# Longer warming, earlier raw weights, two more large tiles and joined read-backs at the start of an FFT and two expert layers

## The chip, the cores and the metric

One core of a Trainium2 chip runs the whole program. Its engines are TensorE (PE; its weight loads are PEld), VectorE (DVE), ScalarE (ACT), GpSimd (POOL) and SyncE (SP, which here only issues DMA transfers). The metric is the device time of one execution in microseconds.

## The reference

```python
def reference(x, moe_w_in, moe_w_out, moe2_w_in, moe2_w_out, moe2_alpha):
    X = fft(fft(x, axis=1), axis=2).real          # x: (2, 3008, 256)
    x = X.reshape(6016, 256)
    h = x @ moe_w_in                              # 256 x 2048
    x = (h * sigmoid(h)) @ moe_w_out              # 2048 x 256
    h = x @ moe2_w_in
    return (max(h, 0) + moe2_alpha * min(h, 0)) @ moe2_w_out
```

A two-dimensional Fourier transform of each of two batches (only its real part is kept) is followed by an expert layer with SiLU and one with a leaky rectifier whose slope differs by column.

## The kernel before, in words

**The transform.** 3008 is 64 times 47. Stage A folds the input (mirrored rows and columns are added and subtracted on VectorE and GpSimd) and multiplies by the 64-point cosines and sines (`psa`); the result `ya` is written to memory as `ys`, in three parts of the output index (`K_PARTS`: 12, 12 and 8 of 32) for each of two halves `h`, and is read back in another layout as `y`, since stage B needs 96 other rows on the partitions. In stage B (`psb`) the 47-point transform is done, one small matmul for each output index; its result is split into a high part by ScalarE and a low part by VectorE (`z`). Stage C transforms the 256 columns in three products, `ce`, `co` and `cn`, giving the even and odd parts (`eo`) of a pair of mirrored tokens. A batch has three chunks of 502 pairs.

**The expert layers.** For each chunk and each of 16 blocks of the hidden dimension (96 steps in all) there are six matmuls `pe` and `po`, VectorE forms `t`, `hp = t + po` and `t - po`, ScalarE applies SiLU, one engine takes the low half `gl`, and twelve matmuls add to the output. The first two chunks run side by side, blocks 0 to 7 of each and then 8 to 15. The second layer follows with a scheme of seven products in place of eight.

**Precision and weights.** A product in full precision is made of three matmuls of high and low parts. Weights arrive as 64-bit floats; a raw piece is turned into 32-bit floats by one ScalarE and four VectorE operations (`cvi`, `cvo`; lines 181, 185, 189, 193 and 197). A group of weights `g` is a quarter of the hidden dimension; `load_w1(g)` and `load_o1(g)` load its raw inputs and outputs, `load_half` does it by halves for group 0.

**Order.** The start, up to stage C of chunk 0, is written in order by hand (`manual_schedule`): on each engine, SP's queue included, instructions run in that order. From there a planner with its own estimate of times orders the instructions of the 96 steps; `PLAN` says at which step each piece is put into its list, and it may set an instruction earlier, in the head too. `behind(st, 0)` holds a step's instructions behind chunk 0's last ScalarE step on that engine. `warm` issues matmuls whose result nobody reads, 12 calls of it after stage A; a call in full 32-bit precision is two passes. Large tiles (8 KB in each partition: x, `ya`, `y`, `z`, `eo`, raw weights) share 10 slots of the pool `bp`; a transfer into a tile waits until the tile that had the slot before is no longer used.

The order of SP's queue at the place of the change is: stores of `ys` part 0, first half of raw outputs of group 0, `y` part 0, second half of those, `ys` part 1, `y` part 1, raw inputs of group 1, alpha, `ys` part 2, raw outputs of group 1, `y` part 2.

Of the kernel before, what the change touches and what calls it, by code (L numbers as in the profile page):

```python
# [25 lines left out]
PLAN = {  # L26
# [5 lines left out]
}  # L32
# [15 lines left out]
F_PARTS = (0, 8, 16)  # L48
ORDER = [(c, f) for f0, f1 in zip(F_PARTS, F_PARTS[1:]) for c in range(2) for f in range(f0, f1)]
ORDER += [(c, f) for c in range(2, NC) for f in range(NF)]  # L50
WARM = 12
WARM0 = 8
SUM0 = "vpapap"
I1_AT = 0
# [11 lines left out]
FA0, FR0, R0, RS0, CD0, SD0, SG0, OD0, NCONST = 0, 128, 256, 444, 634, 762, 890, 1018, 1146  # L66


def _tables():
    c = np.zeros((128, NCONST), np.float64)  # L70
    n1 = np.arange(N1)
    th = 2 * np.pi * np.outer(n1, np.arange(33)) / N1
    fa = np.zeros((N1, 64))
    fa[:, :32] = np.cos(th[:, :32])
    fa[:, 32] = np.cos(th[:, 32])
    fa[:, 33:] = np.sin(th[:, 1:32])
    fr = fa.copy()
    fr[:, 1:32] = -fa[:, 33:]
    fr[:, 33:] = fa[:, 1:32]
    for q in range(2):  # L80
        for j in range(2):
            for k0, k1 in zip(K_PARTS, K_PARTS[1:]):
                at = 4 * k0 + (2 * q + j) * (k1 - k0)
                for to, f in ((FA0, fa), (FR0, fr)):
                    c[64 * q : 64 * q + 64, to + at : to + at + k1 - k0] = f[:, 32 * j + k0 : 32 * j + k1]
    n2 = np.arange(24)
    ph = 2 * np.pi * np.outer(n2, np.arange(N2)) / N2
    co, si = np.cos(ph), np.sin(ph)
    row = 4 * (n2 % 12) + 2 * (n2 // 12)
    for h, (re, im) in enumerate(((co, -si), (si, co))):  # L90
        for j in range(2):
            for to, at in ((R0 + 94 * h, 47 * j), (RS0 + 95 * h, 48 if j else None)):
                if at is None:
                    c[row, to : to + 24] = re[:, :24]
                    c[row + 1, to + 24 : to + 48] = re[:, :24]
                else:
                    c[48 * j + row, to + at : to + at + 47] = re
                    c[48 * j + row + 1, to + at : to + at + 47] = im
    m = np.arange(128)
    ps = 2 * np.pi * np.outer(m, m) / D  # L100
    c[:, CD0 : CD0 + 128] = np.cos(ps)
    c[0, CD0 : CD0 + 128] = 1 - m % 2
    c[:, SD0 : SD0 + 128] = -np.sin(ps)
    c[:, SG0 : SG0 + 128] = ((-1.0) ** m)[:, None]
    c[0, OD0 : OD0 + 128] = m % 2
    return c.astype(np.float32)
# [13 lines left out]
def fft_moe_kernel(  # L120
# [12 lines left out]
    nc = tc.nc  # L133
    wp = ctx.enter_context(tc.tile_pool(name="wp", bufs=1))
    dp = ctx.enter_context(tc.tile_pool(name="dp", bufs=1, space=bass.MemoryType.DRAM))
    bp = ctx.enter_context(tc.tile_pool(name="bp", bufs=10))
    ep = ctx.enter_context(tc.tile_pool(name="ep", bufs=3))
    cp = ctx.enter_context(tc.tile_pool(name="cp", bufs=5))
    kp = ctx.enter_context(tc.tile_pool(name="kp", bufs=16))
# [24 lines left out]
    def split(hi, lo, src, lo_eng=None):  # L164
        nc.scalar.activation(hi, src, AF.Copy)
        return (lo_eng or nc.vector).tensor_tensor(lo, src, hi.bitcast(F32), op=ALU.subtract)
# [57 lines left out]
    cs = wp.tile([128, CD0], F32, tag="cs", name="cs")  # L224
    fh = wp.tile([128, 128], F32R, name="fh")
    fl = wp.tile([128, 128], F32R, name="fl")
# [5 lines left out]
    YS = {}  # L232
    Y = {}
# [72 lines left out]
    def load_y(b, h, kh):  # L306
        w = (K_PARTS[kh + 1] - K_PARTS[kh]) // 2
        if (b, kh) not in Y:
            Y[b, kh] = big([96, 2, 6, 128], F32, f"y{b}_{kh}")
        src = YS[b, h, kh].rearrange("n (a j k) m -> j (n a) k m", a=4, j=2)  # L310
        for j in range(2):
            last = nc.sync.dma_start(Y[b, kh][48 * j : 48 * j + 48, h, :w, :], src[j])
        return last

    def stage_b(b, h):
        at = [0]
# [80 lines left out]
    def load_half(key, src, i, at=None):  # L397
        if key not in RAW:
            RAW[key] = big([128, 1024, 2], U32, f"raw_{key}")
        at = i * 512 if at is None else at  # L400
        t = RAW[key].rearrange("p n t -> p (n t)")
        return nc.sync.dma_start(t[:, i * 1024 : i * 1024 + 1024], src[:, at : at + 512].bitcast(U32))
# [9 lines left out]
    def load_w1(g):  # L412
        load_raw(f"i{g}", wi1[0, :, 512 * g : 512 * g + 512], wi1[1, :, 512 * g : 512 * g + 512])

    def load_o1(g):
        load_raw(f"o{g}", wo1[:, 1024 * g : 1024 * g + 1024])
# [361 lines left out]
    def warm(w, x, n):  # L778
        if n == 0:
            return  # L780
        ps = mm_ps("warm")
        for j in range(n):
            nc.tensor.matmul(ps[:, : x.shape[1]], w, x, start=True, stop=True)

    if True:
        with tc.manual_schedule():
            zero = conv(F32, "zero")
            nc.vector.memset(zero[:, :256], 0.0)
            warm(zero[:, :128], zero[:, :256], WARM0)
            nc.vector.memset(sm, 0.0)  # L790
            nc.scalar.activation(sm[:1, :1], sm[:1, :1], AF.Silu)
            for j in range(len(PIECES) - 1):
                load_x(0, j, (PIECES[j + 1] - PIECES[j]) // 2)
                if j == 0:
                    nc.sync.dma_start(cs[:, :R0], cst[:, :R0])
            cc = conv(F32, "cc")
            for g in range(2):
                load_half("i0", wi1[g], g, 0)
                if g == 0:
                    nc.sync.dma_start(cc, cst[:, CD0:])  # L800
                    nc.sync.dma_start(w128_raw.rearrange("p n t -> p (n t)"), w128.bitcast(U32))
            nc.sync.dma_start(cs[:, R0:], cst[:, R0:CD0])
            fold, mm, rest = stage_a(0)
            (i00, _), (i01, after_i0) = prep_w1(0)
            for (h, i), n in zip(A_ORDER, A_WARM):
                if h == 0:
                    fold(i)
                mm(h, i)
                warm(cs[:, FA0 : FA0 + 128], cs[:, :256], n)
            load_half("o0", wo1, 0)  # L810
            for h in range(2):
                load_y(0, h, 0)
            load_half("o0", wo1, 1)
            warm(cs[:, FA0 : FA0 + 128], cs[:, :256], WARM)
            (s0, p0), (s1, p1) = prep_o1(0)
            w128_st = to_f32(lambda: w128_sb, ("w128", 0, NF), "w128")[1]
            run(i00[:4])
            run(i01[:2])
            run(w128_st[:1])
            nc.scalar.activation(ch, cc, AF.Copy)  # L820
            run(i00[4:])
            for ab in zip(i01[2:], w128_st[1:]):
                run(ab)
            run(w128_st[4:])
            nc.vector.tensor_tensor(cl, cc[:, : SG0 - CD0], ch.bitcast(F32)[:, : SG0 - CD0], op=ALU.subtract)
            for n, (st, pool) in enumerate(zip(after_i0, SUM0)):
                (st if callable(st) else st[pool == "v"])()
                if n == 2:
                    run(s0)
            b00, b01 = stage_b(0, 0), stage_b(0, 1)  # L830
            run(b00[:2])
            run(b01[:2])
            run(p0)
            run(s1[:EARLY_O0])
            run(stage_c(0, 0))
            rest(1)
            for h in range(2):
                load_y(0, h, 1)
            load_w1(1)
            nc.sync.dma_start(alpha_sb, alpha)  # L840
            rest(2)
            load_o1(1)
            for h in range(2):
                load_y(0, h, 2)
        n1 = NC * NF
# [9 lines left out]
        def put(a, b, steps):  # L855

            for j, st in enumerate(steps):
                plan.setdefault(a + (b - a) * j // len(steps), []).append(st)
# [5 lines left out]
        def behind(st, *at):  # L864
            with ExitStack() as stack:
                for k in at:
                    stack.enter_context(tc.issue_after(LAST[k].ins))
                run([st])
# [4 lines left out]
                nc.gpsimd.tensor_copy(cx[64 * j : 64 * j + 1, :], ch[:1, OD0 - CD0 : OD0 - CD0 + 128])  # L873

        put(*PLAN["cx"], [mixed_cosines])
        put(*PLAN["fa"], [lambda: split(fh, fl, cs[:, FA0 : FA0 + 128])])
        put(*PLAN["o0"], [lambda st=st: behind(st, 0, ("low", 0)) for st in s1[EARLY_O0:] + p1])
        put(*PLAN["i1"], [lambda st=st: behind(st, 0, ("t", I1_AT)) for st in staged(prep_w1(1))])
        put(*PLAN["o1"], staged(prep_o1(1)))
# [11 lines left out]
        a, b = PLAN["w2"]  # L891
# [19 lines left out]
        with tc.manual_schedule():  # L911
            low1(n1 - 1)
            for n in range(NP + 2):
                run(plan.pop(n1 + n, []))
                t, p = divmod(n, 8)
# [93 lines left out]
```

## Time and profile before

| | |
|---|---|
| median of 3 runs | 984.3 us (981.82 to 985.46) |
| profiled execution | 988.99 us, span 987.2 us |
| TensorE busy | 957.9 us, 97% of the span |
| VectorE, ScalarE, GpSimd busy | 780.8, 710.7, 405.4 us |
| mean granted clock of TensorE | 0.988 of full speed |

The span runs from the first instruction to the last one. The granted clock is the share of its full speed that TensorE was given; 1.00 is 2.4 GHz and 0.50 is 1.2 GHz. In the chain of work that ended last, TensorE has 78%, VectorE 9%.

### The profile page before, as it was taken

What the parts mean: (1) busy time and instruction counts of PE and PEld (TensorE: products, weight loads), DVE (VectorE), ACT (ScalarE), POOL (GpSimd) and SP (SyncE); (2) the same over time, 40 slices, a digit from 0 to 9 for tenths busy, and PEclk for the clock granted to TensorE, in tenths of its full rate; (3) what the DMA queues carried; (4) which work ended last, traced back from release to release, by engine and by line L of the source; (5) the groups of instructions that cost most, each with busy time, mean ns of one, the idle gap of its engine ahead of it and who ended that gap; (6) DMA issues with size and microseconds to landing.
All of it is one profiled execution on the core that took longest, in us unless ns stands there. A gap on an engine that the chain in (4) does not pass through costs nothing.

```text
span 987.2 us, 14338 instructions
## 1 busy us (share of the span) xinstructions
PE 957.9 (97%) x5170; PEld 824.7 (84%) x5170; DVE 780.8 (79%) x1328; ACT 710.7 (72%) x1410; POOL 405.4 (41%) x355
## 2 busy tenths in 40 slices
PE   7889899999999999999899999999999999999998
PEld 5768787888878788787789999999999999999997
DVE  6888898676796876958687887878878788787876
ACT  3557566665667666666887888878888788787875
POOL 2677869333257467697641221312213122131200
PEclk9789999999999999999999999999999999999999
DMA  8730300230110201100000000000000000000000
GB/s 264 235 122 3 105 22 1 52 104 1 43 43 9 94 1 43 43 9 35 1 1 22 1 22 22 1 21 1 21 9 14 21 1 21 2 22 21 1 21 21
DMA packets 16614, 37.05 MB, mean 38 GB/s; under 512 B 1824, under 2 KB 11296, under 8 KB 14880
## 3 DMA queue, kind: packets, MB, share of 16 engines
q1 hardware_dynamic: 16544, 36.15, 11.1%
q8 instruction: 40, 0.66, 0.3%
q14 instruction: 30, 0.25, 0.1%
HBM read 26.83 MB, written 9.31 MB: 37 GB/s over the span
## 4 chain that ended last, share of the span: by engine, by line
PE 78%; DVE 9%; issue 5%; POOL 4%; ACT 3%; DMA 1%; SPq 0%; POOLq 0%; ACTq 0%; DVEq 0%
PE a L768 27%; PE ac L670 20%; PE a L610 5%; PE a L612 5%; PE a L608 5%; PE b L670 3%; POOL gl L588 2%; PE po L560 1%; PE po L561 1%; PE pe L560 1%; PE po L562 1%; DVE hp L571 1%; PE pe L562 1%; PE pe L561 1%; PE psb L325 1%
## 5 line engine op out<-in xcount | busy, mean ns | idle before, releaser
L768 PE MATMUL a<-gh,wo 128*128 128x502 f32 x768 | 268.2, 391 | 0.0
L588 POOL TENSOR_TENSOR gl<-t,gh 128x502 fp32r<-128x502 f32 x96 | 131.6, 1371 | 95.1 <-ACT t L576 81.6
L768 PEld LDWEIGHTS a<-gh,wo 128*128 128x128 f32 x768 | 145.0, 189 | 23.2
L737 DVE SCALAR_TENSOR_TENSOR h<-h,fc,q 128x502 f32<-128x502 f32 x192 | 130.3, 679 | 38.4 <-ACT q L732 35.7
L610 PE MATMUL a<-gl,wo 128*128 128x502 f32 x384 | 148.3, 395 | 4.1 <-POOL gl L588 4.1
L768 PE MATMUL a<-gl,wo 128*128 128x502 f32 x384 | 149.7, 391 | 0.0
L612 PE MATMUL a<-gh,wo 128*128 128x502 f32 x384 | 147.3, 393 | 0.0
L748 DVE TENSOR_TENSOR gl<-h,gh 128x502 fp32r<-128x502 f32 x192 | 140.5, 732 | 0.1
L575 ACT ACTIVATE gh<-hp 128x502 fp32r<-128x502 f32 x96 | 59.7, 622 | 92.6 <-DVE hp L571 90.6
L608 PE MATMUL a<-gh,wo 128*128 128x502 f32 x384 | 122.8, 397 | 1.2 <-ACT gh L575 0.8
L743 ACT ACTIVATE gh<-h 128x502 fp32r<-128x502 f32 x192 | 118.5, 617 | 2.1 <-DVE h L737 2.1
L732 ACT ACTIVATE q<-h,fc 128x502 f32<-128x502 f32 x192 | 116.9, 609 | 3.0 <-DVE h L715 1.5
L646 POOL TENSOR_TENSOR xt<-o 128x252 f32<-128x252 f32 x24 | 16.7, 716 | 187.2 <-ACT q L732 131.1
L568 DVE SCALAR_TENSOR_TENSOR t<-n,sm,pe 128x502 f32<-128x502 f32 x96 | 70.2, 731 | 29.0 <-PE pe L562 25.3
L610 PEld LDWEIGHTS a<-gl,wo 128*128 128x128 f32 x384 | 73.2, 191 | 20.7 <-POOL gl L588 5.9
L588 POOL TENSOR_TENSOR gl<-hp,gh 128x502 fp32r<-128x502 f32 x52 | 69.4, 1335 | 47.6 <-ACT hp L576 39.8
L571 DVE TENSOR_TENSOR hp<-t,po 128x502 f32<-128x502 f32 x96 | 64.5, 672 | 29.5 <-PE po L562 23.8
L608 PEld LDWEIGHTS a<-gh,wo 128*128 128x128 f32 x384 | 72.2, 191 | 17.5 <-ACT gh L575 2.2
L612 PEld LDWEIGHTS a<-gh,wo 128*128 128x128 f32 x384 | 73.1, 190 | 15.0
L768 PEld LDWEIGHTS a<-gl,wo 128*128 128x128 f32 x384 | 72.5, 189 | 7.7
L704 ACT ACTIVATE u<-ac 128x252 f32<-128x252 f32 x96 | 36.6, 381 | 51.6 <-PE ac L670 51.6
L656 POOL TENSOR_TENSOR os<-o,os 128x252 fp32r<-128x252 f32 x36 | 32.5, 918 | 94.5 <-ACT os L655 92.6
(191 smaller groups left out, 2296.0 us busy)
## 6 DMA issues: line engine op xcount, KB each, us to landing
out_t<-ot SPq DMA_DIRECT2D x24, 251.0 KB, 2.5
x<-in_xs SPq DMA_DIRECT2D x8, 512.0 KB, 5.6
raw_i<-in_wi SPq DMA_DIRECT2D x8, 512.0 KB, 4.7
raw_w<-in_wi SPq DMA_DIRECT2D x4, 1024.0 KB, 5.0
raw_w<-in_wo SPq DMA_DIRECT2D x4, 1024.0 KB, 4.8
raw_o<-in_wo SPq DMA_DIRECT2D x3, 1024.0 KB, 5.6
y<-ys SPq DMA_DIRECT2D x16, 144.0 KB, 2.9
x<-in_xs SPq DMA_DIRECT2D x2, 1024.0 KB, 4.8
```

What stands on the lines that cost most here:

```text
L568: nc.vector.scalar_tensor_tensor(t, E128[c], w128_sb[:, f : f + 1], pe, op0=ALU.mult, op1=ALU.add)
L571: nc.vector.tensor_tensor(hp, t, po, op=ALU.add)
L588: (nc.gpsimd if s or lo_pool(i + 1) else nc.vector).tensor_tensor(lo, h, hi.bitcast(F32), op=ALU.subtract)
L608: nc.tensor.matmul(ACC1[lb, s], hi, G[i, s][0], start=st, stop=False)
L610: nc.tensor.matmul(ACC1[lb, s], hi, G[i, s][1], start=False, stop=False)
L612: nc.tensor.matmul(ACC1[lb, s], lo, G[i, s][0], start=False, stop=sp)
L670: nc.tensor.matmul(to, w, x, start=start and q == 0, stop=q == 2, skip_group_check=True)
L732: nc.scalar.activation(h["q", i][:, to], source(n, part), AF.Abs, scale=coef(n, i, 1))
L737: nc.vector.scalar_tensor_tensor(h[f"h{i}"][:, to], source(n, part), coef(n, i, 0), h["q", i][:, to], op0=ALU.mult, op1=ALU.add)
L743: nc.scalar.activation(hi, H[n][f"h{i}"], AF.Copy)
L748: nc.vector.tensor_tensor(lo, H[n][f"h{i}"], G[n, i][0].bitcast(F32), op=ALU.subtract)
L768: nc.tensor.matmul(ACC2[lb], w[lb][j], x, start=st and first, stop=sp and last)
```

## The change

- `WARM`, the calls of warming matmuls between stages A and B, goes from 12 to 18.
- The raw weights of group 1, 2 MB in three transfers, are issued right after those of group 0, ahead of the stores of `ys` parts 1 and 2 and the reads of `y` parts 1 and 2.
- The pool of large tiles has 12 slots; the space set aside for DMAs that the program builds at run time is cut to 1,024 bytes.
- `y` is read with one transfer of 96 partitions for each half and part, not two of 48. The rows on the partitions come in another order, and the table of stage B has its rows in that order too.
- The split of stage A's matrix into `fh` and `fl` (for the second batch) is held behind chunk 0.

```diff
--- before.py
+++ after.py
@@ -48,7 +48,7 @@
 F_PARTS = (0, 8, 16)
 ORDER = [(c, f) for f0, f1 in zip(F_PARTS, F_PARTS[1:]) for c in range(2) for f in range(f0, f1)]
 ORDER += [(c, f) for c in range(2, NC) for f in range(NF)]
-WARM = 12
+WARM = 18
 WARM0 = 8
 SUM0 = "vpapap"
 I1_AT = 0
@@ -86,16 +86,16 @@
     n2 = np.arange(24)
     ph = 2 * np.pi * np.outer(n2, np.arange(N2)) / N2
     co, si = np.cos(ph), np.sin(ph)
-    row = 4 * (n2 % 12) + 2 * (n2 // 12)
+    row = n2 % 12 + 48 * (n2 // 12)
     for h, (re, im) in enumerate(((co, -si), (si, co))):
         for j in range(2):
             for to, at in ((R0 + 94 * h, 47 * j), (RS0 + 95 * h, 48 if j else None)):
                 if at is None:
                     c[row, to : to + 24] = re[:, :24]
-                    c[row + 1, to + 24 : to + 48] = re[:, :24]
+                    c[row + 24, to + 24 : to + 48] = re[:, :24]
                 else:
-                    c[48 * j + row, to + at : to + at + 47] = re
-                    c[48 * j + row + 1, to + at : to + at + 47] = im
+                    c[12 * j + row, to + at : to + at + 47] = re
+                    c[12 * j + row + 24, to + at : to + at + 47] = im
     m = np.arange(128)
     ps = 2 * np.pi * np.outer(m, m) / D
     c[:, CD0 : CD0 + 128] = np.cos(ps)
@@ -133,7 +133,7 @@
     nc = tc.nc
     wp = ctx.enter_context(tc.tile_pool(name="wp", bufs=1))
     dp = ctx.enter_context(tc.tile_pool(name="dp", bufs=1, space=bass.MemoryType.DRAM))
-    bp = ctx.enter_context(tc.tile_pool(name="bp", bufs=10))
+    bp = ctx.enter_context(tc.tile_pool(name="bp", bufs=12))
     ep = ctx.enter_context(tc.tile_pool(name="ep", bufs=3))
     cp = ctx.enter_context(tc.tile_pool(name="cp", bufs=5))
     kp = ctx.enter_context(tc.tile_pool(name="kp", bufs=16))
@@ -307,10 +307,10 @@
         w = (K_PARTS[kh + 1] - K_PARTS[kh]) // 2
         if (b, kh) not in Y:
             Y[b, kh] = big([96, 2, 6, 128], F32, f"y{b}_{kh}")
-        src = YS[b, h, kh].rearrange("n (a j k) m -> j (n a) k m", a=4, j=2)
-        for j in range(2):
-            last = nc.sync.dma_start(Y[b, kh][48 * j : 48 * j + 48, h, :w, :], src[j])
-        return last
+        nc.sync.dma_start(
+            Y[b, kh][:, h, :w, :].rearrange("p k m -> p (k m)"),
+            YS[b, h, kh].rearrange("n (a k) m -> a n (k m)", a=8),
+        )
 
     def stage_b(b, h):
         at = [0]
@@ -811,6 +811,8 @@
             for h in range(2):
                 load_y(0, h, 0)
             load_half("o0", wo1, 1)
+            load_w1(1)
+            load_o1(1)
             warm(cs[:, FA0 : FA0 + 128], cs[:, :256], WARM)
             (s0, p0), (s1, p1) = prep_o1(0)
             w128_st = to_f32(lambda: w128_sb, ("w128", 0, NF), "w128")[1]
@@ -836,10 +838,8 @@
             rest(1)
             for h in range(2):
                 load_y(0, h, 1)
-            load_w1(1)
             nc.sync.dma_start(alpha_sb, alpha)
             rest(2)
-            load_o1(1)
             for h in range(2):
                 load_y(0, h, 2)
         n1 = NC * NF
@@ -873,7 +873,7 @@
                 nc.gpsimd.tensor_copy(cx[64 * j : 64 * j + 1, :], ch[:1, OD0 - CD0 : OD0 - CD0 + 128])
 
         put(*PLAN["cx"], [mixed_cosines])
-        put(*PLAN["fa"], [lambda: split(fh, fl, cs[:, FA0 : FA0 + 128])])
+        put(*PLAN["fa"], [lambda: behind(lambda: split(fh, fl, cs[:, FA0 : FA0 + 128]), 0)])
         put(*PLAN["o0"], [lambda st=st: behind(st, 0, ("low", 0)) for st in s1[EARLY_O0:] + p1])
         put(*PLAN["i1"], [lambda st=st: behind(st, 0, ("t", I1_AT)) for st in staged(prep_w1(1))])
         put(*PLAN["o1"], staged(prep_o1(1)))
@@ -988,7 +988,7 @@
         "wo2": bits(rows(moe2_w_out)),
         "alpha": np.ascontiguousarray(moe2_alpha.reshape(NF, 128).T),
     }
-    nc = _bacc.Bacc("TRN2", target_bir_lowering=False, num_devices=1)
+    nc = _bacc.Bacc("TRN2", target_bir_lowering=False, num_devices=1, dynamic_dma_scratch_size=1024)
     args = [
         nc.dram_tensor(
             f"in_{n}", arrays[n].shape, U64 if arrays[n].dtype == np.uint64 else F32, kind="ExternalInput"
```

## Rows read from the trace of the kernel before

**Rows 1.** The page: engine totals, and the digits of the 40 slices.

```profile
...
PE 957.9 (97%) x5170; PEld 824.7 (84%) x5170; DVE 780.8 (79%) x1328; ACT 710.7 (72%) x1410; POOL 405.4 (41%) x355
...
PEclk9789999999999999999999999999999999999999
...
```

**Rows 2.** Windows (stretch, length, busy time of PE, PEld, DVE, ACT, POOL, clock, DMA, GB/s).

```profile
...
8.00:12.00 4.00, 2.98 (x8) 1.35 (x8) 3.37 (x6) 1.19 (x2) 1.99 (x2) 1.00 1.00 396
...
25.00:28.00 3.00, 3.00 (x14) 3.00 (x14) 2.82 (x4) 0.55 (x3) 2.92 (x3) 0.50 0.95 283
...
40.00:45.00 5.00, 2.76 (x16) 2.18 (x15) 4.97 (x10) 3.59 (x8) 4.88 (x8) 1.00 0.89 290
...
45.00:50.00 5.00, 4.66 (x25) 3.70 (x23) 5.00 (x9) 2.57 (x6) 4.03 (x4) 1.00 0.36 115
...
55.00:60.00 5.00, 3.46 (x8) 2.82 (x9) 4.76 (x9) 3.38 (x8) 5.00 (x5) 0.55 0.59 210
...
100.00:110.00 10.00, 6.97 (x29) 5.54 (x28) 10.00 (x11) 2.72 (x6) 7.50 (x7) 0.84 0.17 73
...
```

**Rows 3.** Timeline of TensorE, 16 to 44 us (start, duration, line, tile, count, idle).

```profile
...
16.18 5.43 PE L783 MATMUL warm<-cs 128*128 128x256 f32 x24
...
25.00 3.27 PE L325 MATMUL psb<-cs,y 96*128 96x95 f32 x14 [3.40 <-DMA y<-ys]
...
34.94 0.45 PE L560 MATMUL pe<-eo,wi 128*128 128x502 f32 x1
...
40.59 0.83 PE L325 MATMUL psb<-cs,y 96*128 96x94 f32 x6
...
43.66 0.49 PE L610 MATMUL a<-gl,wo 128*128 128x502 f32 x1 [2.24 <-POOL gl L588]
...
```

**Rows 4.** Timeline of VectorE, 25 to 62 us.

```profile
...
25.89 1.64 DVE L197 SCALAR_TENSOR_TENSOR cvo<-raw_o,cvo 128x512 uint32<-128x512 uint32 x1
...
36.16 0.73 DVE L568 SCALAR_TENSOR_TENSOR t<-n,sm,pe 128x502 f32<-128x502 f32 x1
...
62.02 0.68 DVE L571 TENSOR_TENSOR hp<-t,po 128x502 f32<-128x502 f32 x1 [2.25 <-PE po L562]
...
```

**Rows 5.** Groups of VectorE, 27.4 to 36.2 us (busy, mean | idle before them).

```profile
...
L345 DVE TENSOR_TENSOR z<-psb,z 128x283 fp32r<-128x283 f32 (+2 forms) x6 | 1.9, 348 | 2.6 <-ACT z L343 2.6
...
L185 DVE TENSOR_SCALAR cvo<-cvo 128x512 f32<-128x512 f32 x1 | 1.1, 1050 | 0.6 <-ACT cvo L181 0.6
...
L166 DVE TENSOR_TENSOR eo<-co,eo 128x502 fp32r<-128x502 f32 x1 | 0.7, 680 | 0.3 <-ACT eo L165 0.3
...
```

**Rows 6.** Timeline of VectorE and TensorE, 98 to 107 us.

```profile
...
98.86 2.89 DVE L185 TENSOR_SCALAR cvi<-cvi 128x512 f32<-128x512 f32 x2
...
106.93 0.79 PE L560 MATMUL po<-eo,wi 128*128 128x502 f32 x1 [3.03 <-DVE t L568]
...
```

**Rows 7.** Timeline of SP's DMA queue, 20 to 32 us.

```profile
...
20.48 1.71 SPq L312 DMA_DIRECT2D y<-ys  x4
...
22.70 0.97 SPq L295 DMA_DIRECT2D ys<-ya  x2
...
29.11 2.60 SPq L312 DMA_DIRECT2D y<-ys  x4
...
31.82 0.83 SPq L393 DMA_DIRECT2D raw_i<-in_wi  x2
...
```

**Rows 8.** DMA issues at 22 to 33 us (count, KB each, us to landing).

```profile
...
ys<-ya SPq DMA_DIRECT2D x2, 288.0 KB, 6.5
...
y<-ys SPq DMA_DIRECT2D x4, 144.0 KB, 2.6
...
raw_i<-in_wi SPq DMA_DIRECT2D x2, 512.0 KB, 5.5
...
```

**Rows 9.** Timeline of VectorE in the head, 7 to 10 us.

```profile
...
7.06 0.96 DVE L166 TENSOR_TENSOR fl<-cs,fh 128x128 fp32r<-128x128 f32 x1 [0.53 <-ACT fh L165]
...
9.91 0.69 DVE L258 TENSOR_TENSOR x<-x 128x512 f32<-128x512 f32 x1 [0.58 <-DMA x<-in_xs]
...
```

## The prediction

> **What bounds the kernel now.** I read the page first. TensorE is busy 97% of the span, and the clock digits are 9 nearly everywhere; what is lost lies in the first tenth and in a few dents [rows 1]. So a change to the start can only win what TensorE stands idle, or runs at half clock, before it is saturated. I then cut the start into windows. From 25 to 28 us TensorE's granted clock is 0.50, the lower level of 1.2 GHz, although it is busy the whole time; the same low level comes back in most of 55 to 60 us (0.55) and in part of 100 to 110 us (0.84) [rows 2]. The timeline of TensorE tells why the first fall comes: the warming matmuls run from 16.18 to 21.61 us, then TensorE idles 3.40 us until y, read back from memory, has landed, and starts stage B at 25.00 us at half clock; the first matmul of the expert loop starts at 34.94 us [rows 3]. Last I read VectorE, because from about 36 to 60 us it is VectorE that has no idle time, while TensorE waits for it: the groups of the stretch from 27.4 to 36.2 us show 2.6, 0.6 and 0.3 us of idle, all behind ScalarE work that itself stands behind stages B and C on TensorE [rows 5]. After its first SiLU input at 36.16 us the next gap of VectorE is the 2.25 us before 62.02 us [rows 4]. So two things set when the loop is under way: TensorE at half clock in stages B and C, and behind it a queue of VectorE work (weight conversions, the low halves, the SiLU inputs) that can't start before stage C delivers.
>
> **Longer warming (12 to 18 calls).** Each call is two passes: 24 passes take 5.43 us, 0.226 us each [rows 3]. 36 passes take 8.15 us and end at 16.18 + 8.15 = 24.33 us. If y lands as now, the gap is 0.67 us in place of 3.40. Does that hold the clock? A gap of 2.24 us before 43.66 us left the clock at 1.00 through the following matmuls; one of 3.03 us before 106.93 us is followed by a window with 0.84 [rows 2, 3, 6]. 0.67 us is well below both. I take it as held. The extra passes cost nothing, since TensorE has no other work before y lands; if y landed before 24.33 us they would delay stage B by the difference, at most 0.67 us.
>
> **What the held clock is worth.** On TensorE: 25.00 to 34.94 us is 9.94 us at half clock, so at most 4.97 us. The matmuls themselves show the ratio: 14 passes of stage B in 3.27 us at half clock, 0.234 us each, against 6 in 0.83 us at full clock, 0.138 us each [rows 3]. But VectorE then binds. It ends the conversion that stands ahead of stage B's low halves at 27.53 us (25.89 + 1.64), whatever TensorE does [rows 4]. Behind it, up to the first SiLU input at 36.16 us, it is idle for 2.6 + 0.6 + 0.3 = 3.5 us in five gaps [rows 5]. That is the most that can be taken out, and at full clock each of the five waits falls: the first group of stage B is six passes, 0.83 us, and the twelve of half 0 some 1.7 us, so they are done by 26.7 us, before VectorE is free. So the SiLU input moves from 36.16 to 32.7 us, and since VectorE has no idle time from there to about 60 us, the whole queue moves by the same 3.5 us. Bounds: 0 (if the clock falls) and -4.97 us; I take -3.5, because it is VectorE's queue that ends last here.
>
> **Raw weights of group 1 ahead of y's parts 1 and 2.** They were issued from 31.82 us on, behind the wait for y's part 1 at 29.11 us [rows 7], and landed after 5.5 us, at 37.3 us [rows 8], just behind the first SiLU input. With that input at 32.7 us the conversions behind it would wait for them until 37.3 us; so this edit takes away the wait that would be next. It needs two free large tiles, which 12 in place of 10 give (a cost of nothing but space). What it costs is SP's queue and the transfers: 2,097,152 bytes now stand ahead of the stores of ys part 1 (issued at 22.70 us, landing after 6.5 us) on which part 1 of y waits [rows 7, 8]. The best rate in the windows is 396 GB/s, that of 25 to 28 us 283 GB/s [rows 2]: 5.3 to 7.4 us more. y's part 1 would be issued at 33.5 to 36.5 us in place of 29.11 (0.86 us of issue is saved by the joined transfers), and would land 2.6 us later or more [rows 8], at 36 to 40 us. Who waits: the psb matmuls of chunk 1, now at 40.59 us and at about 37.1 when moved. A wait of 0 to 2.9 us on TensorE; 2.24 us of idle stands right behind those matmuls already, waiting for GpSimd [rows 3], which covers most of it. I take 0 and keep +0.7 as the upper end if the order stays. y's part 2 is wanted far later.
>
> **One transfer for each half and part.** Four issues of 1.71 us become two, so half 0's only issue ends 0.43 us earlier [rows 7]. Whether one transfer of 96 partitions moves as fast as two of 48 no row shows. 294,912 bytes at 396 GB/s are 0.74 us; at half that rate 1.49 us. So half 0 lands between 0.43 us earlier and 0.3 us later, half 1 up to 1.1 us later. Both ends are hidden: VectorE is not free before 27.53 us, so stage B may start 0.8 us later without moving it. I take 0.
> The Trainium skill speaks against this edit: "DMA: Bandwidth & Descriptors", section "Why a DMA increments its semaphore by 16 and not by 1", says that a transfer uses the largest number of engines up to 16 that divides the slowest dimension of both sides; the new source's slowest dimension is 8, that of the old ones 48. By that rule the slow end holds, and the sum stays as it is; no row of before has such a transfer.
>
> **The split of the stage A matrix (fh, fl) behind chunk 0.** Now it sits in the head, 0.96 us on VectorE at 7.06 us [rows 9]. Taken away there it wins nothing: the next fold waits for x to land at 9.91 us anyhow [rows 9]. Put behind chunk 0 it meets a VectorE that is full from 32.7 us on: 0 (if the planner sets it after 62 us) to +0.96 us (as long as now). Without GpSimd beside it, it should be shorter; I take +0.3. The table's new row order and the smaller scratch cost nothing: the instructions that use them are the same.
>
> **Sum.** -3.5 + 0.3 = -3.2 us: 988.99 to 985.8 us for the profiled execution. The median of the runs is 4.7 us below that execution, and I carry the difference over: 984.3 - 3.2 = 981.1 us.
>
> **Rivals.**
> (a) More comes of it, 0.27. The planner orders everything from the loop on anew. For it: at 55 to 60 us the clock is 0.55 and VectorE then waits 2.25 us for TensorE; if the fall isn't repeated, this goes too. At 98 to 107 us two conversions take 2.89 us a pair on VectorE while GpSimd works, TensorE idles 3.03 us and then runs at half clock, in all about 4.7 us (3.03 + 0.16 x 10) [rows 2, 4, 6]. Either gone: 976.4 to 978.9 us. Against: the same work has to be done by the same engines.
> (b) y's part 1 comes late and takes the place of the wait removed, 0.12: +0.8 to +2.7 us, 981.9 to 983.8 us. It decides if part 1 lands after about 38 us.
> (c) The longer warming doesn't hold the clock, 0.05: a transfer that runs on fewer DMA engines brings half 0 so late that the gap is over 2.24 us, which needs a landing after 26.6 us. Then everything is as before, with stage B up to 1.1 us later and the +0.3: 985.7 us. The rule above would make this likelier; the 0.3 us that it costs by the rows doesn't reach it.
> (d) The other side, 0.14: the new order makes another collision of conversions on VectorE and GpSimd like that at 98 us. Raw weights that come earlier, with two tiles more, are what lets the planner pull conversions together. One costs 4.7 us, 981.1 + 4.7 = 985.8 us; from two on the kernel is clearly slower, 990.5 us. It decides as soon as one is added without another going.
>
> **How the numbers follow.** My forecast, 0.42, has 978.5 to 983.5 us as its own range (fl and y at their ends, the clock's phase). 0.5% of 984.3 is 4.9 us, about what a measurement of this kernel can tell from no change: the bounds are 979.4 and 989.2. Faster: all of (a) and the low sixth of mine, 0.34. Slower: a third of (d) and a rest, 0.06. Same: 0.60. The range, from the middle of (a) with both its gains to (d) with one collision, is 975.5 to 986.0 us.
>
> **What would show it.** The warming matmuls end near 24.3 us; stage B starts near 25 us with a granted clock of 1.00 through 35 us; the first matmul of the loop starts near 31 us and VectorE's first t near 32.7 us; no wait of psb for y at 36 to 40 us; each y transfer of 288 KB lands in about the time of two of 144 KB. I am wrong if the clock is 0.50 again after 25 us, if psb waits over 2 us for y, or if the 3.5 us are there at 60 us and gone at 500 us: then it is the planner's order, not the start.

## The result and the profile after

The changed kernel takes 991.96 us (median of 4 runs, 990.87 to 993.7); beside it the kernel before took 983.62 us (981.82 to 985.46). The ratio is 1.0086, 95% interval [1.0061, 1.0112]: slower by 8.3 us, where 3.2 us less was forecast. The median is outside the range, 975.5 to 986.0. The profiled execution takes 990.87 us, its span is 989.1 us, the mean clock 0.992.

The page of the changed kernel has TensorE as busy as before [rows 1], and a lower digit of the clock only in the second slice:

```profile
...
PE 958.5 (97%) x5182; PEld 822.2 (83%) x5182; DVE 778.5 (79%) x1328; ACT 711.0 (72%) x1410; POOL 404.7 (41%) x355
...
PEclk9899999999999999999999999999999999999999
...
```

So the loss is in the start again. TensorE's timeline there:

```profile
...
15.28 8.02 PE L783 MATMUL warm<-cs 128*128 128x256 f32 x36
...
24.16 1.55 PE L325 MATMUL psb<-cs,y 96*128 96x95 f32 x12 [0.87 <-ACT wi L432]
...
26.04 0.43 PE L325 MATMUL psb<-cs,y 96*128 96x95 f32 x2 [0.32 <-DMA y<-ys]
...
30.37 0.39 PE L560 MATMUL pe<-eo,wi 128*128 128x502 f32 x1
...
45.41 0.79 PE L610 MATMUL a<-gl,wo 128*128 128x502 f32 x1 [7.57 <-POOL gl L588]
...
```

The first four rows are close to what was forecast, though the whole start comes 0.9 us earlier than in the kernel before (the warming begins at 15.28 us, not at 16.18): the longer warming ends at 23.30 us, the gap of 3.40 us is 0.87 [rows 3], a second one of 0.32 us stands before half 1, and the expert loop begins at 30.37 us in place of 34.94. VectorE's first SiLU input follows at 32.76 us (32.7 forecast, 36.16 before [rows 4]):

```profile
...
32.76 0.73 DVE L568 SCALAR_TENSOR_TENSOR t<-n,sm,pe 128x502 f32<-128x502 f32 x1
...
```

The last row of TensorE has the loss: 7.57 us of idle for the low half `gl` from GpSimd, 2.24 us before [rows 3]. Windows (columns as in [rows 2]) show it, with the fall of the clock behind it:

```profile
...
25.00:28.00 3.00, 2.68 (x22) 2.34 (x21) 2.70 (x5) 1.32 (x5) 2.78 (x2) 1.00 0.96 321
...
28.00:31.00 3.00, 2.95 (x12) 1.80 (x10) 2.14 (x6) 2.91 (x7) 1.30 (x1) 1.00 1.04 411
...
37.00:40.00 3.00, 0.84 (x4) 0.37 (x3) 3.00 (x8) 0.46 (x1) 0.00 (x0) 1.00 0.67 196
...
40.00:45.00 5.00, 0.00 (x0) 0.00 (x0) 2.40 (x5) 0.00 (x0) 4.14 (x6) 0.63 0.41 124
...
45.00:50.00 5.00, 4.58 (x14) 3.98 (x15) 0.84 (x2) 1.25 (x3) 2.20 (x5) 0.50 1.00 379
...
```

From 40 to 45 us TensorE does nothing at all and GpSimd only begins; then the clock is at its lower level, 1.2 GHz (0.50), for 45 to 50 us. GpSimd's own timeline says what it waited for:

```profile
...
29.02 1.30 POOL L454 TENSOR_TENSOR wo<-cvo,wo 128x512 fp32r<-128x512 f32 x1 [1.25 <-ACT wo L450]
...
40.85 1.61 POOL L483 TENSOR_SCALAR fc<-sm 128x16 f32<-128x16 f32 x1 [10.53 <-DMA sm<-in_alpha]
...
44.12 1.24 POOL L588 TENSOR_TENSOR gl<-hp,gh 128x502 fp32r<-128x502 f32 x1
...
```

It stands idle 10.53 us for `sm`, the tile that alpha is loaded into. `fc` is part of the coefficients of the second layer, first read by another engine at 330.36 us, by ScalarE; the planner sets these small operations into the start, ahead of `gl`, on a queue that runs in order. SP's queue tells why alpha is late:

```profile
...
19.37 1.58 SPq L310 DMA_DIRECT2D y<-ys  x2
...
21.48 1.02 SPq L393 DMA_DIRECT2D raw_i<-in_wi  x2
...
23.70 1.29 SPq L295 DMA_DIRECT2D ys<-ya  x2
...
33.78 1.45 SPq L310 DMA_DIRECT2D y<-ys  x2
...
35.28 0.45 SPq L841 DMA_DIRECT2D sm<-in_alpha  x1
...
```

Alpha's transfer, 8 KB, is issued behind the read of `y` part 1. That read waits for the stores of `ys` part 1, which now move behind 2 MB of raw weights; so it is issued at 33.78 us (29.11 before [rows 7]), and alpha at 35.28 us, used at 40.85 us. In the kernel before alpha was only just in time. A further execution of that kernel (B1 below) has on GpSimd:

```profile
...
39.05 0.20 POOL L483 TENSOR_SCALAR fc<-sm 128x16 f32<-128x16 f32 x1 [0.23 <-DMA sm<-in_alpha]
...
41.20 1.69 POOL L588 TENSOR_TENSOR gl<-hp,gh 128x502 fp32r<-128x502 f32 x1
...
```

There the wait for alpha was 0.23 us and the first `gl` began at 41.20 us; in the changed kernel it begins at 44.12 us, while the first SiLU input, from which its own inputs come, was done 3.4 us earlier than before. The transfer had no slack to lose.

### The profile page after: what moved, and what is told of

It reads as the page before. It is cut to its first block, busy times and chain, and to the rows that moved or that the text cites. A ratio compares the mean times of both kernels' runs of the same rounds, so it can differ in the third digit from the quotient of the medians.

```text
span 989.1 us, 14341 instructions
## 1 busy us (share of the span) xinstructions
PE 958.5 (97%) x5182; PEld 822.2 (83%) x5182; DVE 778.5 (79%) x1328; ACT 711.0 (72%) x1410; POOL 404.7 (41%) x355
## 4 chain that ended last, share of the span: by engine, by line
PE 82%; DVE 6%; POOL 4%; issue 3%; ACT 2%; DMA 2%; SPq 1%; POOLq 0%; DVEq 0%; ACTq 0%
PE a L768 26%; PE ac L670 20%; PE a L610 7%; PE a L612 6%; PE a L608 6%; PE b L670 3%; PE po L560 2%; PE pe L560 2%; PE po L562 2%; PE pe L562 2%; PE po L561 2%; PE pe L561 2%; POOL gl L588 1%; DMA ys<-ya 1%; PE psa L281 1%
```

## The experiments

**E1: alpha first.** The changed kernel with alpha's transfer ahead of the raw weights of group 1. The order on TensorE, VectorE and ScalarE is that of the changed kernel.

```diff
             load_half("o0", wo1, 1)
+            nc.sync.dma_start(alpha_sb, alpha)
             load_w1(1)
...
-            nc.sync.dma_start(alpha_sb, alpha)
             rest(2)
```

> The changed kernel, with the 8 KB transfer of alpha issued ahead of the raw weights of group 1 in place of behind y's part 1. The orders of TensorE, VectorE and ScalarE stay the same. Theory A (GpSimd's coefficient steps wait for alpha in front of the low halves, and TensorE waits 7.57 us for these): about 992 - 7.5 = 984.5 us, and the wait of TensorE near 45 us is gone. Rival B (the loss comes from the planner's new order, which pulls the conversions of group 1 ahead of the SiLU inputs on VectorE): 990 to 992 us. Rival C (y's part 1 comes late behind 2 MB of weights): 988 to 992 us, with TensorE waiting for y near 38 us.

988.35 us (6 runs), ratio to the kernel before 1.0047 [1.003, 1.0065]: 3.6 us of the 8.3 are gone by the medians (the intervals of the two overlap a little), and so is the wait of 7.57 us. Not all, since in its profile the clock falls early again:

```profile
...
25.38 1.55 PE L325 MATMUL psb<-cs,y 96*128 96x95 f32 x12 [1.79 <-ACT wi L432]
...
27.53 0.71 PE L325 MATMUL psb<-cs,y 96*128 96x95 f32 x2 [0.61 <-ACT z L343]
...
```

And its windows:

```profile
...
28.00:31.00 3.00, 3.00 (x15) 2.67 (x15) 0.45 (x1) 0.50 (x2) 2.16 (x4) 0.50 1.03 403
...
31.00:34.00 3.00, 3.00 (x8) 2.38 (x8) 2.00 (x5) 2.05 (x5) 2.89 (x5) 0.50 0.90 296
...
```

The gaps are 1.79 and 0.61 us, and the clock is 0.50 from 28 to 34 us, where the changed kernel, with the same warming and gaps of 0.87 and 0.32 us, had 1.00. The first gap is put down to a ScalarE instruction that had ended at 24.43 us, 0.95 us earlier; the other thing that stage B waits for is the read of `y`, so it is the read that landed late.

**E2: the coefficients held behind `gl`.** Alpha stays where the change puts it; the six coefficient steps are put behind a later `gl` on GpSimd. In the trace they run from 319.4 us on.

```diff
...
+            if s:
+                LAST["gl"] = r
...
-        put(*PLAN["co"], [coefficients])
+        put(*PLAN["co"], [lambda: behind(coefficients, "gl")])
```

> The changed kernel, with GpSimd's six coefficient steps held behind the low half of step 58 or so; every transfer is issued as in the changed kernel, and the orders of TensorE, VectorE and ScalarE are the same. Theory A: the same gain as with alpha early, about 984.5 us, although alpha itself lands as late as before. If the place of alpha in the queue mattered for another reason than GpSimd's order (rival C), this would stay at 988 to 992 us. Rival B: 990 to 992 us.

987.9 us (7 runs), 1.0038 [1.0024, 1.0052]: as E1, by the other way round. Alpha late does no harm by itself; what stood behind it on GpSimd did. Here too the gaps before stage B, 1.35 and 0.67 us, are longer, and the clock falls, from 28 to 31 us. E2 issues its transfers in the changed kernel's order, and still stage B starts 5.11 us after the read of `y` is issued (19.72 us), where the changed kernel has 4.79: so part of this gap differs from one execution to the next.

**E3: only the longer warming, in the kernel before** (`WARM = 18`).

> The kernel before with 18 warming calls alone. The instruction orders are those of before. My forecast's step (the clock falls in every execution of the kernel before and a longer warming holds it): 983.6 - 3.5 = about 980 us. Rival D (the fall at 25 us belongs to the profiled execution, which at 988.99 us was some 5 us over the median of the timed ones): 983 to 984 us, no change.

983.78 us (11 runs), 0.9995 [0.9985, 1.0004]: 0.5 us is seen of the 3.5, and 1.5 at most by the interval. Its windows say where the rest went:

```profile
...
25.00:28.00 3.00, 3.00 (x25) 2.65 (x24) 2.84 (x6) 1.77 (x7) 2.88 (x2) 1.00 0.82 261
...
34.00:37.00 3.00, 1.76 (x7) 0.72 (x5) 1.72 (x4) 1.89 (x4) 1.28 (x1) 1.00 1.03 321
...
37.00:40.00 3.00, 2.60 (x10) 2.02 (x9) 2.97 (x7) 2.03 (x6) 2.50 (x6) 0.60 0.97 372
...
40.00:45.00 5.00, 4.34 (x15) 3.75 (x15) 5.00 (x8) 3.28 (x8) 4.07 (x5) 0.56 0.84 263
...
```

The clock is held at 25 to 37 us. Then VectorE is busy 1.72 of 3.00 us from 34 to 37 us, since ScalarE waits 1.11 us for the raw weights of group 1 and VectorE 1.25 us behind it, as the forecast said of this case; TensorE runs dry too, and the clock falls at 37 to 45 us in place of 25 to 34.

**E4: the changed kernel with 12 calls of warming.**

> The changed kernel with 12 warming calls again. With theory A the time is set by alpha's arrival, which the warming doesn't move, so up to some 4 us of a later loop start hide in front of it: 991 to 993 us. If the warming is worth its 3.5 us in the changed kernel as it stands: about 995.5 us.

995.06 us (4 runs), 1.0113 [1.01, 1.0126]. I had expected it hidden under GpSimd's wait; it costs 3.1 us by the medians, though the intervals of the two overlap a little. In its profile the wait is shorter and still ends later:

```profile
...
47.51 0.79 PE L610 MATMUL a<-gl,wo 128*128 128x502 f32 x1 [5.99 <-POOL gl L588]
...
```

Alpha is used at 40.82 us, as in the changed kernel, but GpSimd then takes longer up to the end of `gl`: 2.08 us for one coefficient step, 1.74 for `wo` and 1.69 for `gl`, where the changed kernel has 0.27, 1.26 and 1.24. So the later start isn't hidden. Why these steps are longer wasn't tested.

**E5: E1 with the two reads of 48 partitions.**

> The changed kernel with alpha early, and with y read again by two transfers of 48 partitions for each half and part (and the table rows that go with it). Theory Y (the joined transfer lands half 0 later, so the gap after the warming grows to 1.4 to 1.8 us and the clock falls all the same): the gap is below 1 us, the clock stays at 1.00 from 25 to 34 us, and the time falls from 988.2 to 984 to 985 us. Theory B (the planner's order with the raw weights ahead costs the rest): 987 to 988 us, with the clock held at the start but the matmuls behind in the stretch from 34 to 60 us.

985.55 us (12 runs), 1.0012 [1.0002, 1.0022]: 2.8 us less than E1. One gap of 1.10 us, clock 1.00 from 25 to 40 us. By this one profile, what is left of the 3.5 us is lost at VectorE, which is busy all the time from 31 to 50 us; TensorE waits for it, and the clock falls again:

```profile
...
36.43 0.50 PE L608 MATMUL a<-gh,wo 128*128 128x502 f32 x1 [1.26 <-ACT gh L575]
...
41.41 0.91 PE L325 MATMUL psb<-cs,y 96*128 96x94 f32 x6 [1.51 <-DVE t L568]
...
```

And the windows of E5:

```profile
...
40.00:45.00 5.00, 3.00 (x11) 2.11 (x12) 5.00 (x11) 1.52 (x3) 0.09 (x1) 0.73 0.69 199
...
45.00:50.00 5.00, 4.70 (x14) 3.21 (x14) 5.00 (x8) 3.00 (x7) 3.63 (x3) 0.50 1.00 412
...
```

**E6: only the joined read, in the kernel before** (with its table).

> The kernel before with the joined transfer of y alone. Theory Y: half 0 lands 0.2 to 0.9 us later and half 1 later still; in the kernel before the clock has time to fall in the gap anyway, so +0.3 to +1.5 us, 985 to 986 us. My forecast's step (hidden behind VectorE): no change, 984.5 us.

986.85 us (12 runs), 1.0023 [1.0013, 1.0034]: the joined read alone costs 2.3 us. Its timeline of TensorE:

```profile
...
24.50 2.46 PE L325 MATMUL psb<-cs,y 96*128 96x95 f32 x12 [3.33 <-ACT cvo L181]
...
28.19 0.71 PE L325 MATMUL psb<-cs,y 96*128 96x95 f32 x2 [1.24 <-DMA y<-ys]
...
```

And of SP's queue:

```profile
...
20.07 1.57 SPq L310 DMA_DIRECT2D y<-ys  x2
...
```

Two issues take 1.57 us, four took 1.71 [rows 7]: each costs 0.79 us, not 0.43, so nearly nothing is saved on SP, and half 1 lands 1.24 us after TensorE is through with half 0, whose 12 passes already run at a lower clock (2.46 us; 1.55 in the changed kernel).

**E7: E5 with the split of `fh`, `fl` not held; E8: E7 with the conversions of group 1's raw outputs held behind a SiLU input.**

```diff
-        put(*PLAN["o1"], staged(prep_o1(1)))
+        put(*PLAN["o1"], [lambda st=st: behind(st, ("t", 1)) for st in staged(prep_o1(1))])
```

> The kernel of e5 with the split of the stage A matrix where it was before (in the head). If holding it behind chunk 0 costs VectorE time in the busy stretch: 0.3 to 1 us under e5. If it is hidden: the same as e5 within 0.5 us.

> The kernel of e7 (two reads, alpha early, raw weights ahead, 18 warming calls, 12 large tiles) with the conversions of group 1's output weights held on VectorE behind the SiLU inputs of step 1. Theory B (weights that are there early let the planner set eight conversion steps ahead of the SiLU inputs of steps 0 to 2, so TensorE waits for those): the matmuls of the loop come sooner between 34 and 50 us, 983 to 984.3 us against 985.3. Rival E (the order there costs nothing, because the conversions have to be done in that stretch in any case): 985 to 985.6 us.

E7: 985.27 us (12 runs), 1.0008 [0.9998, 1.0017], not to be told from E5. In its profiled execution the clock falls at the start (0.85 from 25 to 28 us, then 0.58) behind a gap of only 0.89 us, shorter than E5's 1.10; and with 983.68 us it is the fastest of E7's twelve runs:

```profile
...
24.52 1.88 PE L325 MATMUL psb<-cs,y 96*128 96x95 f32 x14 [0.89 <-ACT wi L432]
...
28.00:31.00 3.00, 3.00 (x11) 2.48 (x11) 1.52 (x5) 1.89 (x5) 3.00 (x4) 0.58 1.02 412
...
```

E8: 984.35 us (11 runs), 1.0001 [0.9991, 1.0011]; its clock is 1.00 up to 45 us, and still it is no faster than the kernel before.

**B1: the kernel before, once more.**

> The kernel before once more, for a profile of an execution near its median. If the clock falls at 25 us in every execution (my forecast's reading): granted clock 0.50 from 25 to 36 us again. Rival D (that fall belonged to the execution profiled first): a clock of 1.00 there and a time near 984 us.

985.9 us, one run. The clock is 0.65, 0.50 and 0.72 in the windows of 25 to 34 us: the fall that the warming is to prevent is there again. Its clock also falls where that of the first execution did not, behind the wait for the first `gl` (0.79 from 40 to 45 us); the matmul takes 0.79 us in place of 0.49 [rows 3]:

```profile
...
42.95 0.79 PE L610 MATMUL a<-gl,wo 128*128 128x502 f32 x1 [2.21 <-POOL gl L588]
...
```

**E9: E6 with a source that is contiguous** (96 rows of one dimension, and a table to suit).

```diff
...
-            YS[b, h, kh].rearrange("n (a k) m -> a n (k m)", a=8),
+            YS[b, h, kh].rearrange("n (a k) m -> (n a) (k m)", a=8),
```

> The kernel before with one transfer of y for each half and part as in e6, but with the rows on the partitions in the order of memory, so that the source is 96 rows one behind the other and not 8 groups of 12. Theory F (the joined transfer of the changed kernel runs on fewer DMA engines because its source's outermost dimension is 8): half 1 lands without a wait near 28 us, and the time is that of before, 984 to 985 us. Rival G (a transfer of 96 partitions is slower than two of 48 as such): 986.5 to 987 us as in e6.

985.94 us (12 runs), 1.0014 [1.0002, 1.0025]. On SP the two issues take half the time of E6's:

```profile
...
20.41 0.79 SPq L310 DMA_DIRECT2D y<-ys  x2
...
```

There is no second wait for half 1, but stage B starts 1.45 us later than in E6 (25.95 us against 24.50), and the time can't be told from E6's. The windows of 22 to 25 us show how many of the 16 DMA engines are busy while `y` is moved (the share is the last figure but one): the kernel before, E6 and E9.

```profile
...
22.00:25.00 3.00, 0.00 (x0) 0.03 (x1) 1.71 (x5) 1.79 (x3) 2.50 (x4) 0.97 0.84 240
...
22.00:25.00 3.00, 0.50 (x4) 0.53 (x5) 1.68 (x4) 1.81 (x3) 2.83 (x5) 0.99 0.63 150
...
22.00:25.00 3.00, 0.00 (x0) 0.00 (x0) 1.72 (x4) 1.81 (x3) 2.57 (x4) 1.00 0.81 202
...
```

**E10** puts this read into E8, **E11** puts it, 18 calls of warming and alpha ahead of the raw weights into the kernel before.

> The kernel of e8 with the contiguous read of e9. Theories B and F: the same as e8 or up to 0.5 us less, 982.5 to 984.3 us. Rival G: 2 us over e8.

> The kernel before with 18 warming calls, alpha issued early and the contiguous read, the raw weights of group 1 where they were. If the raw weights ahead are worth their place: 0.5 to 2 us over e10. Theory B (the order that they bring costs what their early landing wins): 982.5 to 984 us, the same as e10 or less.

E10: 987.93 us (6 runs), 1.0036 [1.0022, 1.005], some 3.4 us more than E8, though its start is in order: the gap before stage B is 0.38 us and the clock 1.00 from 25 to 45 us.

```profile
...
24.12 1.84 PE L325 MATMUL psb<-cs,y 96*128 96x95 f32 x14 [0.38 <-ACT cvo L181]
...
```

The edit joins batch 1's reads of `y` too, issued from 191 to 320 us. In the two traces TensorE's matmuls come in the same order up to 278 us and in another from there on; level at 257 us, the profiled execution of E10 ends 1.5 us after E8's (spans of 984.1 and 982.6 us). E11: 985.69 us (12 runs), 1.0009 [0.9997, 1.0021], no gain. Its clock is 1.00 from 25 to 37 us behind two gaps:

```profile
...
24.49 1.55 PE L325 MATMUL psb<-cs,y 96*128 96x95 f32 x12 [1.21 <-ACT wi L432]
...
26.68 0.43 PE L325 MATMUL psb<-cs,y 96*128 96x95 f32 x2 [0.65 <-ACT z L343]
...
```

**E12 and E13: the two more tiles.** E12 takes them out of E8 (10 slots), E13 puts them, with the smaller scratch, into E3.

> E8 with 10 large tiles in place of 12; nothing else differs. In E8 the first x tiles of batch 1 load from 62.8 us, against 95.95 in the kernel before, and E8 loses its lead over the kernel before between 60 and 160 us. Theory 1 (the two more tiles let the loads of batch 1 and the conversions of later weights start early, and the planned order then puts that work in front of the matmuls' inputs): the lead of some 1 to 2.5 us is kept, 982.0 to 983.5 us, about 0.9985 of the kernel before. Theory 2 (the lead is lost in the order that the planner writes whatever the tiles are, or to the clock): 984.4 us, 1.000. Theory 3 (the tiles help: with fewer, loads come late): 985.5 us or more.

> E3 (the kernel before with 18 rounds of warming) with 12 large tiles in place of 10. Theory 1 (the tiles cost what E8 lost): 985 to 986 us, 1.001 to 1.002 of the kernel before, against 0.9995 in E3. Theory 2 (the tiles change nothing that lasts): 983.8 us, as E3. Theory 3 (the tiles help): 982.5 us.

E12: 985.26 us (11 runs), 1.0003 [0.9995, 1.0012]; E13: 983.36 us (12 runs), 0.9986 [0.9975, 0.9996]. So the tiles aren't what E8 loses its lead to. A window from 130 to 170 us shows part of the loss, first of E8:

```profile
...
130.00:170.00 40.00, 37.65 (x162) 29.79 (x162) 35.68 (x49) 25.46 (x46) 34.45 (x31) 1.00 0.00 1
...
```

Of E12:

```profile
...
130.00:170.00 40.00, 37.35 (x162) 29.77 (x161) 34.28 (x48) 24.25 (x44) 34.56 (x31) 1.00 0.04 14
...
```

And of E13:

```profile
...
130.00:170.00 40.00, 40.00 (x176) 32.61 (x175) 35.15 (x51) 24.80 (x46) 34.85 (x31) 1.00 0.00 1
...
```

With the raw weights ahead (E8, E12) TensorE is idle 2.35 to 2.65 us from 130 to 170 us, whether the tiles are 12 or 10; with them in their old place (E13) it is never idle there. The two largest of TensorE's waits from 60 to 170 us in E12, by what was waited for (us in total, times, longest):

```profile
...
PE a L608 <- ACT gh L575: 2.5, 2, 1.4
...
PE a L610 <- POOL gl L588: 1.6, 2, 0.9
...
```

And the only one in E13:

```profile
...
PE po L560 <- DVE t L568: 3.0, 1, 3.0
...
```

E13's one wait is the old one at 98 to 107 us [rows 6]; E12's are new ones, for `gh` and `gl`. Moving three transfers on SP's queue makes the planner write another order for every engine.

**The change as a ladder.** Each row has one edit more than the row above it, the first one more than the kernel before:

| kernel | edit added | ratio to before |
|---|---|---|
| E3 | 18 calls of warming | 0.9995 [0.9985, 1.0004] |
| E13 | 12 tiles, smaller scratch | 0.9986 [0.9975, 0.9996] |
| E7 | raw weights and alpha ahead | 1.0008 [0.9998, 1.0017] |
| E5 | `fh`, `fl` held | 1.0012 [1.0002, 1.0022] |
| E1 | joined read | 1.0047 [1.003, 1.0065] |
| after | alpha behind `y` part 1 | 1.0086 [1.0061, 1.0112] |

E13 is the one kernel here that comes out ahead of the kernel before, by 0.14%, and its interval just leaves out no change; its step from E3 alone is not clear. Of the steps, those to E7 and to E1 have intervals that don't overlap; that to the changed kernel overlaps a little, and E2, clear of the changed kernel, confirms it.

## Why the prediction was wrong

**The step that failed** is the second, the raw weights ahead of `y`'s further parts, where it says "Who waits: the psb matmuls of chunk 1". The landing time was right (issue at 33.78 us, 33.5 to 36.5 forecast), and so was it that these matmuls hardly mind. But I asked who waits for `y` part 1 and not what else stands behind its read on SP: alpha, and behind alpha GpSimd's queue with the coefficients and `gl`. In its place TensorE waited 7.57 us for `gl`, a wait that the sum did not have. By E1 and E2, which undo it from the two ends and agree, that costs 3.6 to 4.1 us. By E13 and E7 putting the transfers ahead costs some 2 us more even with alpha out of the way. E8, E12 and E13 show waits of another order in its place, 60 to 170 us; for E7 itself, whose waits there are only 0.8 us longer than E13's, the rest of the 2 us stays open.

**The joined read, taken at 0, costs 2.3 us alone (E6) and 2.8 us in the change (E1 to E5).** The term was mis-sized. The issue that I counted as saved isn't (0.79 us each in place of 0.43), and half 1 comes 1.24 us after TensorE is through with half 0. By the rule of the Trainium skill that I set against it ("DMA: Bandwidth & Descriptors", "Why a DMA increments its semaphore by 16 and not by 1") the source with 8 as its slowest dimension moves on fewer engines than one with 96. The traces agree: from 22 to 25 us the busy share of the DMA engines is 0.63 with 8 (E6), 0.81 with 96 (E9) and 0.84 in the kernel before, and with 96 the wait for half 1 is gone. But E9's time is no better within the intervals, so that the engines are the cause isn't shown. Nor is it the start alone: E10, with the clock held and a gap of 0.38 us, loses 3.4 us against E8. I sized the reads of batch 0's part 0 and left out batch 1's, which the edit joins too, and the other order that the planner then writes. How the cost divides between the start and that stretch stays open.

**The longer warming** did what was forecast to the gap, the clock, the loop's start and the first SiLU input. Its worth, -3.5 us, was right only for the first 10 us: E3 gives -0.5 us at the end. That the first SiLU input came at 32.76 us, 0.06 from the forecast, is in part luck: the conversion ahead of it ended at 26.66 us and not at 27.53, and VectorE still waited 0.30, 0.28 and 0.55 us, which I had put at nothing. I let the whole queue move by what its head won. But VectorE's inputs did not come 3.5 us earlier (E3 waits for raw weights), or it was full and TensorE had to wait for it (E5), and in their profiles TensorE fell to half clock further on, from 37 us (E3) and from 40 to 45 us (E5), in place of 25 us. Whatever the start wins, a planned order further on can give back: E8 has no fall before 45 us and ends level with the kernel before. In the changed kernel without the longer warming (E4) its 3.1 us are seen.

I also took 2.24 us of idle as harmless to the clock, from one gap of the kernel before [rows 3]. That was no ground: in B1, the same kernel, a gap of 2.21 us at the same place is followed by a fall. Nor does the gap before stage B decide alone. With 36 passes of warming the clock held behind 0.85 us (E3), 1.21 us (E13) and 1.21 and 0.65 us (E11), and fell behind 0.89 us (E7), 1.35 and 0.67 us (E2), and 1.79 and 0.61 us (E1). These are single executions, and no limit comes out of them.

**The split** was about right: 0.29 us on VectorE (35.27 us) where +0.3 was forecast, and E5 against E7 can't tell it from nothing.

**The rivals.** (d) came nearest in sign, and partly in kind: a new order with new waits is in E7 and E8, but no second collision of conversions made it. (b), `y` part 1 late, named the right transfer and the wrong one who waits. (c) is seen in the profiled executions of E1, E2 and E7, behind shorter gaps than I required. (a) didn't come.

## What to carry to other kernels

When a transfer is moved on an in-order queue, list every transfer behind it up to the next one that waits, and for each the first instruction that uses it, on whatever engine; a table wanted some 290 us later can stop an engine now, if a planner has hoisted what reads it. A small load that nobody is waiting for belongs ahead of any transfer that waits for another. And a gain at the head of a long planned order is measured at its end: rerun the order with that one edit alone before counting it.

## What the runs showed that I had not expected

- The time to issue a transfer depends on its source's shape: 0.79 us each for 8 groups of 12 rows (E6), 0.40 us for 96 contiguous rows (E9) of the same bytes, 0.43 us for one transfer of 48 rows, half the bytes [rows 7].
- 8 KB of alpha took nearly as long as 512 KB of raw weights (5.5 us to landing [rows 8]): issued by 35.73 us, used at 40.85 us.
- Nearly the same gap was followed by a fall of the clock in one execution and not in another: a fall behind 2.21 us in B1, none behind 2.24 us in the first execution of the same kernel [rows 3]; a fall behind 0.89 us in E7, none behind 1.21 us in E13.
